# Unnormalised band, sums divided out at the readout, and first x as fp32 over one queue: a fused convolution and gated FFN on one Trainium2 core

## Chip, core and metric

One core of a Trainium2 chip runs the kernel. The metric is device time in microseconds (us) of one execution. Of the kernel before, three runs gave 765.75, 765.9 and 766.1 us.

## What is computed

`x` is 8 sequences of 4096 tokens with 192 channels. A causal convolution with 7 taps, one set of taps for each of 8 heads of 24 channels, is followed by a gated feed-forward layer with 1536 hidden channels. The taps are a softmax over the 7 weights of a head.

```python
w = np.exp(weight - np.max(weight, axis=-1, keepdims=True))
w = w / (np.sum(w, axis=-1, keepdims=True) + 1e-09)
...
out = np.einsum('hk,bskhg->bshg', w, x_unf)        # 7 taps, group = D // H = 24
...
gate = np.maximum(x @ w_gate, 0.0)
val = x @ w_val
return (gate * val @ w_out).astype(np.float32)
```

## The kernel before

The eight sequences are two streams of four (sequence b and b + 4 side by side). The work goes in 16 units of 1024 tokens of both streams, each of two windows of 512. For a window, `gate_val` (L528) runs twelve blocks f of 128 hidden channels. A block is 12 matmuls (L541): three channel blocks c of 64 channels, two streams, gate and val; the two streams use the upper and lower half of the array, so the weights `Wg` and `Wv` are held twice, in partitions 0 to 63 and 64 to 127. ACT takes the ReLU of gate (L552), DVE multiplies by val (L553). `project` (L636) multiplies by `Wo` (L570) and ACT and DVE evict.

The convolution of most tokens runs on DVE, ACT and POOL as products and sums with the taps (`lane_first`, `lane_rest`, `product`, `add`), one unit ahead. The first unit has nothing ahead of it, so its convolution runs on PE, as matmuls with a **band matrix**: x in token-major form (`x_h`) is the weight and the band, 118 x 112 with the 7 taps along its diagonals, one for each head, is the moving operand; the result comes out channel-major. Its first window is `first_block` (L387), the second window `second_block` (L394, in front of block f = 5), and the tail of unit 1 is `conv(2)` (L403) with `conv_out` (L421). A window of the first block is cut in 5 token steps jj: step 0 has 96 tokens, steps 1 to 4 have 104 each.

The order of work is written by hand: every engine runs its instructions in the order of the program text, and waits on semaphores. All psum tiles come from one pool of 4 buffers (L71). What stands before the first gate matmul:

- **Taps and band** (L249 to L299): SP loads the weights; DVE takes the maximum (L251), ACT the exp (L254), DVE the sum, the reciprocal and `over`, the reciprocals on a diagonal (L258 to L261). An fp32 matmul of exp and `over` (L272) spreads the normalised taps over 112 partitions; DVE multiplies them into `diag` (L282); 14 matmuls (L292) shift them into the band in psum; `fill_band` (L323) copies it to SBUF as 16 bit.
- **x of the first window**: SP loads steps 1 to 4 of stream 0 as fp32 in one transfer (L122, 336 KB) and step 0 of both streams (L138); ACT (L317) and DVE (L335) cast them to 16 bit. POOL loads steps 1 to 4 of stream 1 with the cast in the transfer (L127).
- **POOL's queue**: after that issue, a mask (L128), and then the issues of the weight pieces s = 0 to 5 (`load_w`, L167) and of x for the second block (`load_x(1)`), with copies of the upper halves (`pool_halves`, L179) between. DVE makes the upper halves of pieces 0 and 1 (`both_halves`, L175), which serve block 0 and blocks 1 and 2; POOL those of piece 2 (blocks 3 and 4) and up.
- **Warm-ups** (L152): matmuls on constants, seven ahead of the taps' matmul and two more between.
- **Taps for the lane** (L303 to L314): ACT scales the exps; ten SP transfers spread them over partitions (`tap`); POOL copies them to the other half (L665). They are read from unit 1's convolution on.

In the first block, channel block 0 takes stream 0 of steps 1 to 4, then stream 1, then step 0; channel blocks 1 and 2 follow. Each block is read from psum to `xc` by one copy of 512 columns (L392): blocks 0 and 2 by ACT, block 1 by DVE.

## Time and profile before

| what | us |
|---|---|
| median of three runs | 765.9 |
| profiled execution, first to last instruction (span) | 764.4 |
| PE busy | 760.3 |
| DVE busy | 705.6 |
| ACT busy | 600.9 |
| POOL busy | 378.4 |
| first convolution matmul starts at | 5.65 |
| first gate matmul starts at | 7.66 |

The profile gives one execution. Its rows have a line of the kernel, an engine, an operation, the tile written and the tiles read; PEld is the loading of weights into PE, which runs beside its matmuls. An idle time in brackets is followed by what ended it. The granted TensorE clock is shown as 9 tenths or more in every slice of the page.

### The profile page before, as it was taken

Reading aid. Unit: us, or ns where it says so; the run is one execution under the profiler, and the core shown is the slowest. Engines: PE = TensorE matmul, PEld = TensorE weight load, DVE = VectorE, ACT = ScalarE, POOL = GpSimd, SP = SyncE. Lnnn points to the kernel's source line nnn. Section 1 sums busy time; section 2 is a strip of 40 time slices with the busy share of each in tenths; the row PEclk is TensorE's granted clock in tenths of the full one; section 3 lists DMA queues with packets and bytes.
Section 4 is the critical chain, followed back from the end, with each engine's and each line's share of the span. In section 5 each row is a group of like instructions: output and inputs, shape, how many; then the busy total and the mean of one; then the engine's idle time right before and its main releaser. Section 6 shows DMA issues by size and latency. Waiting matters only on the chain.

```text
span 764.4 us, 25103 instructions
## 1 busy us (share of the span) xinstructions
PE 760.3 (99%) x10929; PEld 501.3 (66%) x10929; DVE 705.6 (92%) x763; ACT 600.9 (79%) x735; POOL 378.4 (50%) x244
## 2 busy tenths in 40 slices
PE   9999999999999999999999999999999999999998
PEld 5494674947649476584855848567494674947648
DVE  7998999999999999999999999999999999999891
ACT  6787887878878887887878878787787887876571
POOL 9419448093571926729175390853909347090000
PEclk9999999999999999999999999999999999999999
DMA  9969039290452805528073271722819134220202
GB/s 123 134 102 148 7 96 81 65 111 22 95 67 83 97 23 107 49 85 94 30 112 40 85 94 44 120 16 90 89 44 125 13 97 60 66 48 15 71 1 84
DMA packets 131830, 56.00 MB, mean 73 GB/s; under 512 B 96392, under 2 KB 131720, under 8 KB 131720
## 3 DMA queue, kind: packets, MB, share of 16 engines
q1 hardware_dynamic: 90680, 38.81, 23.9%
q0 software_dynamic: 40896, 15.50, 20.3%
q8 instruction: 85, 1.39, 0.8%
q14 instruction: 25, 0.20, 0.1%
q10 hardware_dynamic: 144, 0.10, 0.0%
HBM read 31.48 MB, written 25.17 MB: 74 GB/s over the span
## 4 chain that ended last, share of the span: by engine, by line
PE 99%; DVE 0%; ACT 0%; issue 0%
PE ps L541 65%; PE ps L570 32%; PE ps L619 1%; PE ps L377 0%; PE ps L154 0%; PE ps L411 0%; DVE band L329 0%; PE ps L272 0%; ACT acc L596 0%; PE ps L292 0%
## 5 line engine op out<-in xcount | busy, mean ns | idle before, releaser
L553 DVE TENSOR_TENSOR hT<-gr,ps 128x1024 f16<-128x1024 f16 (+1 forms) x386 | 469.0, 1216 | 36.6 <-ACT gr L552 9.4
L552 ACT ACTIVATE gr<-ps 128x1024 f16<-128x1024 f32 (+1 forms) x386 | 392.9, 1019 | 101.9 <-PE ps L541 99.7
L491 POOL TENSOR_TENSOR prods<-prods 128x1344 f32<-128x1344 f32 x70 | 212.4, 3034 | 290.0 <-DVE prods L487 286.7
L541 PE MATMUL ps<-xc,Wg 64*128 64x512 f16 x2304 | 311.9, 376 | 0.0
L541 PE MATMUL ps<-xc,Wv 64*128 64x512 f16 x2304 | 311.9, 376 | 0.0
L570 PEld LDWEIGHTS <-hT 64*128 64x128 f16 x5952 | 245.9, 94 | 3.7
L570 PE MATMUL ps<-Wo,hT 64*128 64x192 f16 x5952 | 248.1, 243 | 0.0
L541 PEld LDWEIGHTS <-Wv 64*128 64x128 f16 x2304 | 129.8, 94 | 118.5 <-DVE hT L553 0.3
L541 PEld LDWEIGHTS <-Wg 64*128 64x128 f16 x2304 | 112.3, 94 | 132.8 <-issue 0.2
L515 DVE SCALAR_TENSOR_TENSOR acc<-x_r,tap,acc 128x576 f32<-128x576 f16 x225 | 165.3, 813 | 0.0
L485 ACT ACTIVATE prods<-x_r,tap 128x448 f32<-128x448 f16 x222 | 130.1, 660 | 0.0
L596 ACT COPY out_s<-ps 128x768 f32<-128x768 f32 (+1 forms) x64 | 45.5, 711 | 51.3 <-PE ps L570 40.0
L203 POOL DMA_DIRECT2D x_e<-in_x_dram x58 | 47.0, 823 | 16.6 <-ACT acc L501 12.8
L465 POOL COPY x_p<-x_e 128x960 f16<-128x960 f16 (+1 forms) x58 | 50.3, 906 | 1.2 <-DMA x_e<-in_x_dram 1.1
L491 POOL TENSOR_TENSOR xc<-prods 128x1344 f16<-128x1344 f32 x14 | 42.4, 3029 | 1.1
L515 DVE SCALAR_TENSOR_TENSOR xc<-x_r,tap,acc 128x576 f16<-128x576 f16 x45 | 34.1, 813 | 0.0
L501 ACT ACTIVATE acc<-x_r,tap 128x576 f32<-128x576 f16 x45 | 31.4, 763 | 0.0
L487 DVE TENSOR_SCALAR prods<-x_r,tap 128x448 f32<-128x448 f16 x70 | 26.6, 450 | 0.0
L596 DVE COPY out_s<-ps 128x384 f32<-128x384 f32 (+1 forms) x16 | 8.7, 541 | 11.9 <-PE ps L619 9.4
L619 PE MATMUL ps<-Wo,hT 128*128 128x192 f16 x96 | 8.1, 246 | 0.0
L619 PEld LDWEIGHTS <-hT 128*128 128x128 f16 x96 | 7.9, 98 | 0.2 <-issue 0.2
L154 PE MATMUL ps<-const-bfloat16-1.0 128*128 128x512 bf16 (+1 forms) x9 | 3.9, 572 | 0.8 <-PEq L719 0.8
(54 smaller groups left out, 56.3 us busy)
## 6 DMA issues: line engine op xcount, KB each, us to landing
out_dram<-out_s SPq DMA_DIRECT2D x62, 384.0 KB, 2.7
x_e<-in_x_dram POOLq DMA_DIRECT2D x34, 192.0 KB, 7.4
x_e<-in_x_dram POOLq DMA_DIRECT2D x24, 240.0 KB, 5.6
x_r<-x_p SPq DMA_TRANSPOSE x131, 5.1
Wo<-in_moe_w_out_dram POOLq DMA_DIRECT2D x1, 576.0 KB, 7.3
x_h<-in_x_dram POOLq DMA_DIRECT2D x2, 210.0 KB, 4.8
Wg<-in_moe_w_gate_dram POOLq DMA_DIRECT2D x4, 96.0 KB, 4.1
Wv<-in_moe_w_val_dram POOLq DMA_DIRECT2D x4, 96.0 KB, 4.0
```

Source lines behind the costliest of these rows:

```text
L203: first = nc.gpsimd.dma_start(out=xe[:, j0 + start : j0 + n, st, :, :].rearrange("p j c r -> p j (c r)"), in_=bass.AP(tensor=x.tensor, off ...
L465: nc.gpsimd.tensor_copy(out=xp[:, j0 : j0 + n, :, st, :], in_=xe[:, j0 : j0 + n, st, :, :])
L485: engine.activation(out=out, in_=in_, func=ACTF.Copy, scale=scale)
L487: engine.tensor_scalar(out=out, in0=in_, scalar1=scale, scalar2=None, op0=ALU.mult)
L491: nc.gpsimd.tensor_tensor(out=pr[:, 0] if k < KW - 1 else xc[v + 1][:, :, LDVE:UNIT], in0=pr[:, 0], in1=pr[:, k], op=ALU.add,)
L501: nc.scalar.activation(out=accs[v][:, c, :], in_=shifted(v, c, 0, 0), func=ACTF.Copy, scale=tap[:, c, 0:1],)
L515: nc.vector.scalar_tensor_tensor(out=xc[v][:, c, 0:LDVE] if k == KW - 1 else acc[:, c, :], in0=shifted(v, c, k, 0), scalar=tap[:, c, k : k ...
L541: nc.tensor.matmul(out=pss[i][:, st, :], lhsT=W[64 * st : 64 * st + 64, c, 128 * f : 128 * (f + 1)], rhs=xcb[64 * st : 64 * st + 64, c, WI ...
L552: nc.scalar.activation(out=gr[:, sts], in_=pss[0][:, sts], func=ACTF.Relu)
L553: nc.vector.tensor_tensor(out=h[:, f, sts], in0=gr[:, sts], in1=pss[1][:, sts], op=ALU.mult)
L570: mm = nc.tensor.matmul(out=outs[q], lhsT=h[64 * r : 64 * r + 64, f, st, 128 * q : 128 * (q + 1)], rhs=Wo[64 * r : 64 * r + 64, f, :], sta ...
L596: one(out=dst[:, step * j : step * j + step], in_=src[:, step * j : step * j + step])
```

## The change

- The exps go into the band **unnormalised**: ACT writes them as 16 bit (`high`), and a 16-bit matmul with a one-hot matrix spreads them. Sum, reciprocal and `over` are made later; four fp32 matmuls (`spread_scales`) put the reciprocals into all 128 partitions, by channel and by head, and the copies out of psum multiply by them (`by_channel`, and ten scaled copies in `conv_out` in place of five copies).
- `diag` is made in two halves, the band in two psum tiles and copied in four pieces of two heads (before: 3, 1, 2 and 2).
- x of the first window comes **as fp32 by SP alone**: one transfer for each token step of both streams (`load_first`, 168 KB each), in the order 1, 2, 0, 3, 4. Each is cast by one instruction: steps 1 and 3 by ACT, 2 and 4 by DVE, 0 by POOL between its weight issues.
- POOL no longer issues x of stream 1. It makes `owner` and `owners` (a one at each channel's head) with two selects and a copy ahead of the weight issues.
- The first block runs steps 1 and 2 for all three channel blocks, then `spread_scales`, then step 0 with a readout of columns 0 to 303, then the upper halves of weight piece 0 on DVE, then steps 3 and 4 with a readout of columns 304 to 511.
- Four warm-ups of 512 columns stand ahead of the taps' matmul (before: six of 512 and one of 256), 256 columns behind it and 512 behind the band.
- The lane's taps and their ten SP transfers come after the first block.

The diff, without what is only moved:

```diff
-    def body(st):
...
+    def load_first(jj):
+        nc.sync.dma_start(
+            out=stage(0, SUB, 0, 2, jj, 1),
+            in_=bass.AP(
+                tensor=x.tensor,
+                offset=x.offset + (FIRST - PAD + DSUB * (jj - 1)) * D,
+                ap=[[D, SUB], [NB * S * D, 2], [1, D]],
+            ),
         )
 
-    nc.sync.dma_start(out=stage(0, SUB, 0, 1, 1, GSUB - 1), in_=body(0))
+    load_first(1)
+    load_first(2)
+    ones = const.tile([128, 128], FP)
-    nc.gpsimd.dma_start(out=xts[0][0:SUB, 1:GSUB, 1, :], in_=body(1))
...
+    owner = const.tile([H, D], FP)
+    for sign in (1, -1):
+        nc.gpsimd.affine_select(
+            out=owner[:],
+            in_=ones[0:H, 0:1].to_broadcast([H, D]) if sign == 1 else owner[:],
+            pattern=[[sign, D]],
+            compare_op=ALU.is_ge,
+            fill=0.0,
+            base=0 if sign == 1 else G - 1,
+            channel_multiplier=-G * sign,
+        )
+    owners = const.tile([H, NCH, 2, 64], FP)
+    nc.gpsimd.tensor_copy(
+        out=owners[:],
+        in_=owner[:].rearrange("h (c r) -> h c r", r=64).unsqueeze(2).to_broadcast([H, NCH, 2, 64]),
+    )
...
+    load_first(3)
+    load_first(4)
...
     def warm_up(*widths):
-        for n, w in enumerate(widths):
+        for w in widths:
             nc.tensor.matmul(
-                out=warm[:, n % 2, 0:w], lhsT=busy[:, 0:128], rhs=busy[:, 0:w], start=True, stop=True
-            )
-
-    warm_up(512, 512, 512, 512, 512, 512, 256)
+                out=warm[:, 0, 0:w], lhsT=busy[:, 0:128], rhs=busy[:, 0:w], start=True, stop=True
+            )
+
+    warm_up(512, 512, 512, 512)
...
+    def cast(copy, jj):
+        rows = ROWS0 if jj else FIRST + PAD
+        copy(out=xts[0][0:rows, jj, :, :], in_=stage(0, rows, 0, 2, jj, 1))
+
     load_w(0)
-    load_w(1)
+    load_w(1, 1)
+    cast(nc.gpsimd.tensor_copy, 0)
+    load_w(1, 2)
...
+    same = const.tile([SUB, SEG], FP)
+    summed(same[:], pitch_k, SEG, GAP)
+    one_hot = const.tile([H, H], F16)
+    nc.vector.tensor_copy(out=one_hot[:], in_=spaced[0:H, 0, GAP : GAP + H])
     mx = const.tile([H, 1], FP)
     nc.vector.tensor_reduce(
         out=mx[:], in_=wr[:], axis=mybir.AxisListType.X, op=ALU.max, negate=True
     )
+    high = const.tile([H, KW, SEG], F16)
     nc.scalar.activation(
-        ex[:, 0:KW, :], wr[:].unsqueeze(2).to_broadcast([H, KW, SEG]), ACTF.Exp, bias=mx[:]
+        high[:], wr[:].unsqueeze(2).to_broadcast([H, KW, SEG]), ACTF.Exp, bias=mx[:]
     )
+    nc.scalar.activation(ex[:, 0:KW], wr[:], ACTF.Exp, bias=mx[:])
+    summed(places[:, SUB - SEG : SUB - SEG + SEG + KW - 1], pitch_k - 1, SEG + KW - 1, GAP)
+    nc.tensor.matmul(
+        out=warm[0:SUB, 1, 0:H],
+        lhsT=high[:].rearrange("h k s -> h (k s)"),
+        rhs=one_hot[:],
+        start=True,
+        stop=True,
+    )
+    warm_up(256)
+    HB = H // 2
+    diag = const.tile([SUB, H, SEG], F16)
...
+            nc.vector.tensor_tensor(
+                out=diag[:, HB * a : HB * (a + 1)],
+                in0=warm[0:SUB, 1, HB * a : HB * (a + 1)].unsqueeze(2).to_broadcast([SUB, HB, SEG]),
+                in1=same[:].unsqueeze(1).to_broadcast([SUB, HB, SEG]),
+                op=ALU.mult,
+            )
+    bps = [psum.tile([128, 2, 512], FP, name="ps") for _ in range(2)]
...
     sm = const.tile([H, 1], FP)
-    nc.vector.tensor_reduce(out=sm[:], in_=ex[:, :, 0], axis=mybir.AxisListType.X, op=ALU.add)
+    nc.vector.tensor_reduce(out=sm[:], in_=ex[:], axis=mybir.AxisListType.X, op=ALU.add)
+    fill_band(0, [0, 1], nc.vector.tensor_copy)
+    fill_band(0, [2, 3], nc.vector.tensor_copy)
+    fill_band(1, [4, 5], nc.scalar.copy)
+    fill_band(1, [6, 7], nc.scalar.copy)
+    cast(nc.scalar.copy, 1)
+    cast(nc.vector.tensor_copy, 2)
     nc.vector.reciprocal(sm[:], sm[:])
...
+    scales = const.tile([128, NCH + H], FP)
+
+    def spread_scales():
+        for c in range(NCH):
             nc.tensor.matmul(
-                out=(bps, spread)[a][:, a, HB * SEG * b : HB * SEG * (b + 1)],
-                lhsT=places[:, SUB - SEG * (b + 1) : SUB - SEG * (b + 1) + 128],
-                rhs=diag[:, HB * a : HB * (a + 1), :].rearrange("p h s -> p (h s)"),
+                out=bps[1][:, 1, c : c + 1],
+                lhsT=owners[:, c].rearrange("h a b -> h (a b)"),
+                rhs=sm[:],
                 start=True,
                 stop=True,
                 skip_group_check=True,
             )
+        nc.tensor.matmul(
+            out=bps[1][:, 1, NCH : NCH + H],
+            lhsT=ones[0:H, :],
+            rhs=over[:],
+            start=True,
+            stop=True,
+            skip_group_check=True,
         )
+        nc.scalar.copy(out=scales[:], in_=bps[1][:, 1, 0 : NCH + H])
+
+    def scaled(engine, out, in_, scale):
+        if engine is nc.scalar:
+            engine.activation(out=out, in_=in_, func=ACTF.Copy, scale=scale)
+        else:
+            engine.tensor_scalar(out=out, in0=in_, scalar1=scale, scalar2=None, op0=ALU.mult)
+
+    def by_channel(engine, out, in_, c):
+        scaled(engine, out, in_, scales[:, c : c + 1])
...
-    def conv_dense(g, c, ps, bank):
+    def conv_dense(g, c, ps, bank, steps):
...
+        for jj in steps:
...
     def first_block():
-        for c in range(NCH):
-            ps = psum.tile([128, 2, 512], FP, name="ps")
-            conv_dense(0, c, ps, 0)
-            copy = nc.vector.tensor_copy if c == 1 else nc.scalar.copy
-            copy(out=xc[0][:, c, 0:WIN], in_=ps[:, 0, :])
+        xc[0] = xcpool.tile([128, NCH, UNIT], F16, name="xc")
+        place = [(psum.tile([128, 2, 512], FP, name="ps"), 0) for _ in range(NCH)]
+        cut = GROUPS[0][1][3]
+        engines = (nc.scalar, nc.vector, nc.scalar)
+        for steps, done in (((1, 2), None), ((0,), slice(0, cut)), ((3, 4), slice(cut, WIN))):
+            for c, (ps, bank) in enumerate(place):
+                conv_dense(0, c, ps, bank, steps)
+                if done is not None:
+                    by_channel(engines[c], xc[0][:, c, done], ps[:, bank, done], c)
+            if done is None:
+                spread_scales()
+            elif done.start == 0:
+                both_halves(nc.vector.tensor_copy, 0, Wg)
+                both_halves(nc.vector.tensor_copy, 0, Wv)
...
+        conv_dense(1, 0, two, 0, range(GSUB))
+        conv_dense(1, 1, two, 1, range(GSUB))
+        for c in range(2):
+            by_channel(nc.scalar, xc[0][:, c, WIN : 2 * WIN], two[:, c], c)
+        conv_dense(1, 2, one, 0, range(GSUB))
+        by_channel(nc.vector, xc[0][:, 2, WIN : 2 * WIN], one[:, 0], 2)
...
+        for h, (t, bank, slot) in PLACE.items():
+            r = G * h
+            while r < G * (h + 1):
+                c, m = r // 64, min(64 - r % 64, G * (h + 1) - r)
+                scaled(
+                    nc.scalar,
+                    y[0:SUB, 0:n, c, :, r % 64 : r % 64 + m],
+                    wide[t][0:SUB, bank, W * slot : W * (slot + 1)].rearrange(
+                        "p (j s w) -> p j s w", s=2, w=G
+                    )[:, :, :, r - G * h : r - G * h + m],
+                    scales[0:SUB, NCH + h : NCH + h + 1],
+                )
+                r += m
...
     first_block()
+    taps = const.tile([H, KW], FP)
+    nc.scalar.activation(taps[:], ex[:, 0:KW], ACTF.Copy, scale=sm[:])
+    tap = const.tile([128, NCH, KW], FP)
...
+            nc.sync.dma_start(
+                out=tap[r % 64 : r % 64 + n, c, :],
+                in_=taps[h : h + 1, :].unsqueeze(1).to_broadcast([1, n, KW]),
+            )
```

## The prediction

> **What bounds the kernel now.** I read the page first, parts 1 and 4, and then the chain that ended last, in order of time. PE is busy nearly the whole span, and the chain is PE from end to end:

> ```profile
> span 764.4 us, 25103 instructions
> PE 760.3 (99%) x10929; PEld 501.3 (66%) x10929; DVE 705.6 (92%) x763; ACT 600.9 (79%) x735; POOL 378.4 (50%) x244
> PE 99%; DVE 0%; ACT 0%; issue 0%
> ```

> ```profile
> 0.85 2.93 PE ps L154 x7
> 3.78 0.47 PE ps L272 x2
> ...
> 4.79 0.27 PE ps L292 x7
> ...
> 5.09 0.52 DVE band L329
> ...
> 5.65 2.08 PE ps L377 x106
> 7.72 6.66 PE ps L541 x60
> 14.38 1.48 PE ps L377 x120
> 15.86 24.74 PE ps L541 x228
> ...
> 57.46 31.08 PE ps L541 x288
> ```

> Columns: start, length, engine, tile, line. From 7.72 us on PE only multiplies; 288 gate/val matmuls take 31.08 us everywhere, so one block f (12 of them) takes 1.295 us. From there to the end the change removes no matmul, and for the first window PE needs 5 blocks x 1.295 = 6.48 us where the chain shows 6.66. So this change can only move the **time at which gate/val begins** (call it T0; 7.66 in the timeline below), and add or take away stalls in the few blocks behind it, where weights arrive just in time. What lies outside the span is 765.9 - 764.4 = 1.5 us; I keep it, so that the sum, made against the span, carries over to the median.

> The prologue on DVE, ACT and PE (timeline; start, length, what, in brackets the idle time before it):

> ```profile
> 2.10 0.20 ACT L145 ACTIVATE spare<-ones 8x1 f32<-8x1 f32 x1
> 2.19 0.15 DVE L251 TENSOR_REDUCE mx<-wr 8x1 f32<-8x7 f32 x1 [0.47 <-DMA wr<-in_weight_dram]
> 2.37 0.39 ACT L254 ACTIVATE ex<-wr,mx 8x112 f32<-8x112 f32 x1
> ...
> 3.39 0.35 DVE L238 TENSOR_REDUCE same<-spaced 112x16 f32<-112x112 f32 x1
> ...
> 4.29 0.29 DVE L282 TENSOR_TENSOR diag<-ps,same 112x128 f16<-112x128 f32 x1 [0.20 <-PE ps L272]
> ...
> 4.63 0.62 PE L292 MATMUL ps<-diag,places 112*128 112x64 f16 x14
> ...
> 5.09 0.51 DVE L329 CAST band<-ps 128x336 f16<-128x336 f32 x1 [0.51 <-PE ps L292]
> ...
> 5.12 0.92 ACT L317 CAST x_h<-prods 110x256 f16<-110x256 f32 x2 [1.60 <-DMA prods<-in_x_dram]
> ...
> 5.65 2.08 PE L377 MATMUL ps<-band,x_h 110*32 110x104 f16 x120 [0.18 <-DVE band L329]
> 5.67 0.36 DVE L335 CAST x_h<-prods 102x384 f16<-102x384 f32 x1
> ...
> 5.95 0.27 DVE L329 CAST band<-ps 128x112 f16<-128x112 f32 x1
> 5.96 0.58 ACT L329 CAST band<-ps 128x224 f16<-128x224 f32 x2
> 6.18 1.38 PEld L377 LDWEIGHTS <-x_h 110*32 110x32 f16 x104 [0.15 <-DMA x_h<-in_x_dram]
> ...
> 6.86 0.59 ACT L392 CAST xc<-ps 128x512 f16<-128x512 f32 x1 [0.32 <-PE ps L377]
> ...
> 7.66 0.39 PE L541 MATMUL ps<-xc,Wg 64*128 64x512 f16 x2
> ```

> Two waits end late here: the taps' chain (exp, sum, reciprocal, spread, diag, band) lets the convolution begin at 5.65; the second stream's x, loaded by POOL, holds it from 6.0 to 6.18.

> **Part by part: the taps' chain, to the first convolution.** Sum, reciprocal and `over` leave the chain. The exp now feeds a 16-bit matmul directly: exp done at 2.76, or some 0.05 later since `same` (0.35) and a tiny copy now stand ahead of the maximum on DVE, instead of behind `over`. PE has only four warm-ups of 2.93 / 6.5 = 0.45 us ahead, free at 2.65, so the matmul runs at about 2.85 and ends near 3.2. Diag in halves: 0.29 for 128 elements, so about 0.2 for 64: first half 3.45, second 3.6. Fourteen band matmuls: seven take 0.27 us on the chain (39 ns each) at the faster rate, and 64/512 x 0.45 = 56 ns each at the warm-ups' rate; the rate may change among them, so I take 50 ns, 0.7 us for all, and 0.2 us, an estimate, until the last can be read. First half readable near 4.15, second at 4.5.

> ACT then copies band 4-5 and 6-7 (0.58 together) and casts step 1 of x: 384 elements, half of the 768 that took 0.92, so 0.46 to 0.5: 4.55 + 0.58 + 0.47 = 5.6. DVE has its two bands (between 0.27 for 112 and 0.51 for 336, so 0.39 each) and the cast of step 2 (0.36) at 5.2 to 5.3. So the convolution begins at **about 5.6, against 5.65**: the chain is shorter by 0.9 us, but the cast that stood ahead of ACT's bands now stands behind them. x itself is not what holds. The issues of before, with size and time to landing:

> ```profile
> Wv<-in_moe_w_val_dram POOLq DMA_DIRECT2D x4, 96.0 KB, 4.0
> prods<-in_x_dram SPq DMA_DIRECT2D x1, 336.0 KB
> x_h<-in_x_dram POOLq DMA_DIRECT2D x1, 168.0 KB, 4.7
> prods<-in_x_dram SPq DMA_DIRECT2D x1, 144.0 KB, 4.0
> ...
> Wv<-in_moe_w_val_dram POOLq DMA_DIRECT2D x1, 48.0 KB, 3.4
> ```

> Steps 1 and 2 are 336 KB as that first transfer was, which ended ACT's wait at 5.12, and stand in the same place of the same queue. All five transfers read the 816 KB that passed by 6.18 before (POOL's 168 KB were 336 as read); with the weights issued later beside them I put step 4 at 5.9 (5.6 to 6.2) and its cast on DVE at 6.3.

> **Part by part: the convolution and its readout.** PE's order becomes steps 1, 2 (48 matmuls), spread_scales, step 0 (24), steps 3, 4 (48). At 1.48 us for 120, as in the second block, 48 take 0.6: done at 6.2. Then four fp32 matmuls with 128 columns of weights. The one fp32 matmul of before (L272, 112 columns, two records) holds PE for 0.47 at the warm-ups' rate, 0.24 at double rate; four of them 0.9 us. Bounds: 4 x 0.47 = 1.9 us, and 0.5 if weight loads and products of neighbours overlap. I take **0.9: done at 7.1**. This work did not stand in PE's queue before, and everything behind it waits.

> Step 0's cast is on POOL and done by about 6.2 (below), so it is hidden behind this. ACT reads the scales (0.20, as the tiny copy at 2.10) from 7.3 to 7.5. Then channel block 0, columns 0 to 303: 304/512 x 0.59 = 0.35 to 0.4, to 7.95. Steps 3 and 4 write other columns of the same bank, but in the changed program's order of instructions their first matmul for each block waits for that readout's engine. So PE goes on with block 0 at 8.0, 16 matmuls 0.2, 0.2 until readable, then ACT again (it did block 2's first part meanwhile): 208 columns, 0.3: 8.7. **T0 = 8.75 against 7.66, +1.1.** Before, the last convolution of block 0 ended at 6.8 and one copy of 0.59 followed. Block 1 on DVE stands behind both weight copies, block 2 behind block 0 on ACT; they are needed 0.45 and 0.9 us after T0 and come within that.

> **Part by part: POOL and the weights.**

> ```profile
> 1.42 0.88 POOL L127 DMA_DIRECT2D x_h<-in_x_dram  x1 [0.28 <-issue]
> ...
> 2.39 0.36 POOL L128 TENSOR_SCALAR_AFFINE_SELECT spaced<-ones 112x112 f32<-112x112 f32 x1
> ...
> 4.59 0.63 POOL L170 DMA_DIRECT2D Wv<-in_moe_w_val_dram  x1
> ...
> 9.62 6.43 DVE L553 TENSOR_TENSOR hT<-gr,ps 128x512 f16<-128x512 f16 x7 [0.67 <-ACT gr L552]
> ...
> 10.14 0.82 POOL L177 COPY Wv<-Wv 64x768 f16<-64x768 f16 x1
> ...
> 12.27 0.81 PE L541 MATMUL ps<-xc,Wv 64*128 64x512 f16 x6
> ...
> 23.03 0.25 POOL L665 COPY tap<-tap 64x21 f32<-64x21 f32 x1
> ```

> POOL loses the issue of x (0.88) and gains two selects of 192 elements and a copy of 384. Between 0.25 for 21 elements and 0.82 for 768 a straight line gives 0.38 and 0.53; the select of 112 lies 0.04 above it. So 2 x 0.42 + 0.53 - 0.88 = +0.5 (bounds 3 x 0.25 - 0.88 = -0.1 and 3 x 0.82 - 0.88 = +1.6). Behind it the first three weight issues; then the cast of step 0 waits for its x (landed before DVE's cast at 5.67; the same bytes ahead of it in the queue now) and takes 0.53: the issue of the second Wv piece starts at 6.0 against 4.59, **+1.4 for all of POOL's later work**. The upper-half copy of Wv for blocks 3 and 4 ends at 10.96 + 1.4 = 12.4; block 3's val matmuls wanted it at 12.27. With T0 at 8.75 they come at 13.3, so this is hidden; with T0 unchanged it would cost 0.1. DVE's products start at 9.62, behind the ReLU and behind the copy of that second Wv piece; issued at 6.0, it lands 3.4 to 4.0 later, so 9.4 to 10.0, its copy (0.5, by the same line) ends at 9.9 to 10.5. With T0 at 8.75 the first products would start at 9.62 + 1.1 = 10.7. Hidden too; with T0 unchanged up to 0.9 late.

> What else moves is free: the taps and their ten SP issues come behind the first block but are used at 23.03. The second block's two readouts on ACT instead of one, and ten scaled copies instead of five after conv(2), come where ACT waits for PE and not PE for ACT, as at the end of that unit:

> ```profile
> 57.54 0.48 ACT L596 COPY out_s<-ps 128x384 f32<-128x384 f32 x1 [1.23 <-PE ps L570]
> ```

> Five more copies at 0.2 each would be 1.0 us, less than this idle time; without the cover they would cost that.

> **Sum:** +1.1 for T0; of the 0.1 us that blocks 1 to 3 lose now, 0.1 is won back, since DVE and POOL are no longer late. **+1.0: span 765.4, 766.9 us.**

> **The clock at the start.** The warm-ups take 0.45 us per 512 columns, the steady pairs 2 x 31.08/288 = 0.216, and the change of rate falls among the L292 matmuls, near 4.7, after 3.9 us in which PE never stood idle. Now it stands idle from about 2.65 to 2.85 and 3.2 to 3.5; I take it that the rate still changes near 4.7. [...]

> **Rivals.** (1) *Everything as above*: 766.9, from 766.5 to 767.9 by the bounds of the fp32 matmuls (T0 8.35 to 9.75 alone, and 0.3 to either side from transfers). Chance 0.55.

> (2) *The start moves little*: the fp32 matmuls pass in 0.5 us, the first convolution starts 0.3 earlier, and the readouts overlap better. T0 is then about 7.7, and POOL's 12.4 decides: +0.1, 766.0; if the late Wv piece holds DVE as well, up to +0.9, 766.8. For it: it takes only small errors in steps that I added up in a row. Chance 0.2.

> (3) *Faster*: x and the band come early enough that T0 is 7.2, and POOL's delay is under 1.0 (select and copy near 0.25, step 0's x landed before its turn): gain 0.3 to 0.5, 765.5. It decides from a POOL delay under 1.3, since block 3 is held otherwise. Against it: the serial readout alone is 1.5 us long. Chance 0.1.

> (4) *Much slower*: the gaps keep PE at half rate past 5.6. If the 3.9 us of unbroken work that went before the change of rate must be counted anew from 3.5, it comes at 7.4, and half of the 1.8 us since 5.6 is lost: 0.9 on top of +1.0, 767.8. If it lasts through, 48 convolutions cost 0.6 more, the fp32 matmuls 0.95 and the next 40 0.5: 768.9. It decides where the fourteen band matmuls and the first 48 convolutions run at half rate. Chance 0.15.

> **How the numbers follow.** The likeliest is (1), 766.9. The range from 765.6 to 768.2 leaves out about half of (3), a third of (4) and little else. A measurement of this kernel tells about 0.2% (1.5 us, 764.4 to 767.4) from no change. Faster than that would need T0 at 6.1, before the x of the last steps is cast: 0.02. Slower: nearly all of (4) and a fifth of (1), 0.25. Within: 0.73.

> **What would show it.** In the changed profile: the first convolution near 5.6; the four fp32 matmuls holding PE for 0.9 us; each of steps 3 and 4 waiting for ACT or DVE; the first gate matmul at 8.75; the second Wv issue at 6.0 on POOL; from then on blocks of 1.295 us. It is wrong if gate/val begins before 8 us, if blocks 1 to 4 stall, or if the convolution's 120 matmuls run at half rate.

## The result and the profile after

| | before | after |
|---|---|---|
| median, us | 766.02 (765.75 to 766.21) | 771.09 (770.38 to 771.67, five runs) |
| ratio, 95% interval | | 1.0065 [1.0052, 1.0077] |
| profiled execution / its span | 766.1 / 764.4 | 770.38 / 768.7 |
| first convolution matmul / first gate matmul (T0) | 5.65 / 7.66 | 5.68 / 10.84 |

Slower by 5.07 us, where 1.0 was forecast; 771.09 lies above the range. (The 766.1 is inferred: in every run on record that has both, 1.7 us of the time lie outside the span, and of the three runs of before only 766.1 fits 764.4.) The page of after looks as the one of before did: span, PE's busy time, and the granted clock in 40 slices.

```profile
span 768.7 us, 25130 instructions
...
PE 763.1 (99%) x10933; PEld 502.1 (65%) x10933; DVE 706.7 (92%) x767; ACT 602.8 (78%) x745; POOL 379.0 (49%) x247
...
PEclk9999999999999999999999999999999999999999
```

None of it tells what happened: a slice is 19 us long, and matmuls that run more slowly count as busy for longer (a pair of gate matmuls 0.43 us in place of 0.21, below). The chain of waits of after does (start, length, engine, tile, line):

```profile
2.80 0.25 PE ps L291
3.05 0.34 PE ps L175
...
3.41 0.24 DVE diag L303
...
3.69 0.92 PE ps L312 x14
...
4.63 0.59 ACT band L329 x2
5.22 0.42 ACT x_h L244
...
5.68 1.23 PE ps L412 x45
6.92 1.37 PE ps L358 x6
8.29 0.43 PE ps L366 x2
8.72 0.31 PE ps L412 x7
...
9.11 0.52 ACT xc L378
...
9.68 1.23 PE ps L412 x36
10.91 7.47 PE ps L578 x60
18.38 1.48 PE ps L412 x120
```

The second block begins at 18.38 against 14.38: 4.00 us lost by then, 3.19 of them ahead of the first gate matmul (10.91 against 7.72) and 0.81 among the next 60 matmuls (7.47 against 6.66). Nothing is lost after that; the same piece of the chain 500 us later stands 4.00 later too, in before and in after:

```profile
510.82 15.84 PE ps L570 x384
```

```profile
514.82 15.84 PE ps L607 x384
```

The other 0.3 us of the span come behind the last copy out of psum, which starts 4.00 us later too (765.40 against 761.40). The timeline of after shows what the 0.81 us are, and when x and the weights came (idle time before and its end in brackets):

```profile
5.68 1.23 PE L412 MATMUL ps<-band,x_h 110*32 110x104 f16 x48 [0.67 <-ACT x_h L244]
...
5.74 0.50 POOL L244 CAST x_h<-prods 102x384 f16<-102x384 f32 x1 [0.89 <-DMA prods<-in_x_dram]
6.20 0.64 POOL L191 DMA_DIRECT2D Wv<-in_moe_w_val_dram  x1
...
6.46 0.51 ACT L244 CAST x_h<-prods 110x384 f16<-110x384 f32 x1 [0.82 <-DMA prods<-in_x_dram]
...
6.93 0.36 DVE L244 CAST x_h<-prods 110x384 f16<-110x384 f32 x1 [1.41 <-DMA prods<-in_x_dram]
...
10.84 0.61 PE L578 MATMUL ps<-xc,Wg 64*128 64x512 f16 x2
...
12.10 0.64 PE L578 MATMUL ps<-xc,Wv 64*128 64x512 f16 x2
12.52 0.43 PE L578 MATMUL ps<-xc,Wg 64*128 64x512 f16 x2
12.79 0.38 PE L578 MATMUL ps<-xc,Wv 64*128 64x512 f16 x2
13.00 0.81 PE L578 MATMUL ps<-xc,Wg 64*128 64x512 f16 x6
```

A pair of gate matmuls takes 0.43 us from start to start (12.10 to 12.52) until about 12.6 and 0.21 behind it (12.79 to 13.00): **PE ran at half its rate until 12.6 us**, where before it changed near 4.8. The 48 convolution matmuls at 5.68 took 1.23 us, not 0.6. This is rival (4) of the prediction, but longer than that rival allowed.

### The profile page after: what moved, and what is told of

The parts are those of the page before. It is cut to its first block, busy times and chain, and to the rows that moved or that the text cites. A ratio compares the mean times of both kernels' runs of the same rounds, so it can differ in the third digit from the quotient of the medians.

```text
span 768.7 us, 25130 instructions
## 1 busy us (share of the span) xinstructions
PE 763.1 (99%) x10933; PEld 502.1 (65%) x10933; DVE 706.7 (92%) x767; ACT 602.8 (78%) x745; POOL 379.0 (49%) x247
## 4 chain that ended last, share of the span: by engine, by line
PE 99%; ACT 0%; DMA 0%; issue 0%; DVE 0%; ACTq 0%
PE ps L578 65%; PE ps L607 32%; PE ps L656 1%; PE ps L412 1%; PE ps L358 0%; DMA wr<-in_weight_dram 0%; PE ps L312 0%; PE ps L456 0%; ACT band L329 0%; ACT xc L378 0%; PE ps L366 0%; ACT x_h L244 0%; ACT high L286 0%; PE ps L175 0%; ACT acc L633 0%
## 5 line engine op out<-in xcount | busy, mean ns | idle before, releaser
L552 DVE SCALAR_TENSOR_TENSOR acc<-x_r,tap,acc 128x576 f32<-128x576 f16 x225 | 165.3, 812 | 0.0
L552 DVE SCALAR_TENSOR_TENSOR xc<-x_r,tap,acc 128x576 f16<-128x576 f16 x45 | 34.0, 812 | 0.0
L412 PE MATMUL ps<-band,x_h 110*32 110x104 f16 (+7 forms) x240 | 4.7, 247 | 1.0 <-ACT x_h L244 0.7
## 6 DMA issues: line engine op xcount, KB each, us to landing
prods<-in_x_dram SPq DMA_DIRECT2D x4, 168.0 KB, 3.8
```

What stands on the lines that cost most here:

```text
L552: nc.vector.scalar_tensor_tensor(out=xc[v][:, c, 0:LDVE] if k == KW - 1 else acc[:, c, :], in0=shifted(v, c, k, 0), scalar=tap[:, c, k : k ...
```

## What could be the cause, and how it shows

| window that ran at half rate | share, and the run |
|---|---|
| half rate kept | 0.47 and 0.41 (after), 0.76, 0.62, 0.58 (e1), 0.54 (e3), 0.46, 0.74 (e4), 0.72 (e9), 0.70 (e8) |
| full rate granted | 0.82 (before, e8), 0.82 (after, 9.2 to 12.6), 0.78 (e10), 0.85 (e2), 0.87 (e9), 0.89 (e5, e6, e7), 0.90 (e11), 0.93 (e3), 0.96 (e4), 1.00 (e1) |

| window that ran at full rate | share, and the run |
|---|---|
| full rate kept | 0.81 (before), 0.71 (e11), 0.56 (e7), 0.54 (e6), 0.53 (e10), 0.50 (e5) |
| full rate taken away | 0.37 (e2), 0.20 (e8) |

The measure is chosen to fit these windows; the busy time of the profile does not part them. In the window of after from 5.79 to 9.20 PE is busy for 3.41 of 3.41 us, the four fp32 matmuls included, and half rate is kept.

*Theory*: the change opens gaps on PE while it still works at half rate (fewer warm-ups, 0.32 us of waiting for `diag`, 0.67 in front of the convolution, 1.44 us with three fp32 matmuls of one column), so the share is 0.47 and 0.41 in two windows, below the 0.76 behind which e1, too, stays at half rate. *Rivals*: the unnormalised band with its scales is dear by itself; x over one queue comes late; the serial readout.

## The experiments

**e1, e2: fill the gaps in after.** e1 adds warm-ups on both sides; e2 also gives the taps' matmul a psum tile of its own (in after it sits in the warm-up's tile, and `diag` waits for the warm-up behind it).

```diff
-    warm_up(512, 512, 512, 512)
+    warm_up(512, 512, 512, 512, 256)
...
+    spread = psum.tile([128, 2, 512], FP, name="ps")        # e2 alone
-        out=warm[0:SUB, 1, 0:H],
+        out=spread[0:SUB, 0, 0:H],
-    warm_up(256)
+    warm_up(384)                                            # e2 alone
...
-    warm_up(512)
+    warm_up(512, 512, 512)
```

> The changed kernel with more warm-ups: 256 columns more ahead of the taps' matmul, and three instead of one of 512 columns behind the band, so that PE stands idle before the first convolution only for some 0.3 us at 3.4. Theory 'clock' (the idle stretches at 2.7, 3.4 and 5.0 to 5.7 keep PE at half rate until 12.6): the rate doubles by about 6, the four fp32 matmuls take 0.9 instead of 1.80 us, the 48 first convolutions 0.6 instead of 1.23, first gate matmul near 9.0 instead of 10.84, about 767.3. Theory 'added work' (the fp32 matmuls and the split readout cost the same at any rate): no change, 771.

> As e1_fill, and the taps' matmul writes a psum tile of its own instead of a bank of the warm-up tile, so that diag does not wait for the warm-up behind it; that warm-up has 384 columns. PE has no idle stretch over 0.1 us before the first convolution. Theory 'clock': the rate doubles no later than in e1_fill, near 4.8; band 0.3 us earlier, but the casts of x still hold the first convolution near 5.4 to 5.7; about 767.0. Theory 'added work': 770.7 (0.3 for the shorter chain).

Measured: e1 770.02 us, 1.0042 [1.0029, 1.0054], its runs from 767.83 to 771.56. The profiled one is the slowest; in it T0 is 11.04, and the rate changes only at 14.9, against the theory's 6. Its window up to 4.68 had 0.76, and half rate stayed; the lowest share with full rate behind it is e10's 0.78. e2 768.42, 1.0036 [1.0024, 1.0048]: full rate at 4.75, the 48 convolutions 0.66 us (5.56 to 6.22) and the fp32 matmuls 0.98 (6.22 to 7.20). And then the windows of e2 show what neither theory had: columns are stretch, length, busy us (and instructions) of PE, PEld, DVE, ACT and POOL, then the granted clock, the DMA share and GB/s.

```profile
4.80:8.10 3.30, 2.61 (x83) 1.88 (x82) 1.32 (x6) 1.90 (x7) 2.82 (x6) 1.00 1.04 159
8.20:11.50 3.30, 3.30 (x60) 1.76 (x61) 1.91 (x6) 1.36 (x4) 3.26 (x6) 0.50 1.19 134
11.60:15.00 3.40, 3.40 (x36) 1.39 (x32) 2.56 (x5) 3.09 (x5) 3.35 (x6) 1.00 1.37 166
```

The full rate was **taken away again** at 8.16, after a window in which PE waited for ACT's readouts and did fp32 matmuls. So the serial middle of after did not keep the rate that the fills had won. (The first stretch of a trace, ahead of any change of rate, is shown as 1.00 even where it is half: so in before from 1.0 to 4.7, where warm-ups of 512 columns start 0.43 us apart. There only the lengths tell.)

**e3: before, with one gap.**

```diff
-    warm_up(512, 512, 512, 512, 512, 512, 256)
+    warm_up(512, 512, 512, 512)
```

> The kernel before with four warm-ups of 512 columns ahead of the taps' matmul instead of six and one of 256: one edit, PE idle from 2.6 to 3.7, all else as before. Theory 'clock': the rate doubles one or two windows of some 3.4 us later than 4.8, at 8.2 or 11.6; 120 convolutions and the first gate blocks at half rate cost 1.0 to 3.0 us, 767 to 769. Theory 'added work': 766.0, as nothing waits for the removed matmuls.

Measured: 767.08 us, 1.0016 [1.0006, 1.0025]. The timeline of e3:

```profile
3.63 0.51 PE L272 MATMUL ps<-over,ex 8*112 8x8 f32 x2 [0.92 <-ACT taps L304]
...
5.77 3.08 PE L377 MATMUL ps<-band,x_h 110*32 110x104 f16 x120
8.78 0.39 PE L541 MATMUL ps<-xc,Wg 64*128 64x512 f16 x2
```

The same arithmetic as before, and PE idle for 0.92 us: half rate lasts until 8.82, the convolution takes 3.08 us for 2.08, and T0 moves by 1.1. Three warm-ups that compute nothing are worth 1.1 us.

**e4: 16-bit matmuls for the scales, in after.**

```diff
-    owners = const.tile([H, NCH, 2, 64], FP)
+    owners = const.tile([H, NCH, 2, 64], F16)
...
+    sm_h = const.tile([H, 1], F16)
+    nc.vector.tensor_copy(out=sm_h[:], in_=sm[:])
-    over = const.tile([H, H], FP)
+    over = const.tile([H, H], F16)
...
-                rhs=sm[:],
+                rhs=sm_h[:],
-            lhsT=ones[0:H, :],
+            lhsT=ones_h[:],
```

> The changed kernel with the four matmuls that spread the scales in 16 bit instead of fp32 (one-hot matrices, reciprocals and their diagonal rounded to 16 bit; two tiny DVE instructions more). Theory 'added work': the 1.80 us of the four fp32 matmuls fall to about 0.3, 769.6. Theory 'clock': the same 1.5 us in the prologue, and whether the rate doubles earlier depends on what the step counts as activity; if the fp32 matmuls with one column count as idle, the rate doubles at 9.2 instead of 12.6, and some 768.

Measured: 769.22 us, 1.0042 [1.0026, 1.0058]. The timeline of e4:

```profile
6.86 0.23 PE L362 MATMUL ps<-sm_h,owners 8*128 8x1 f16 x3
6.96 0.16 PE L370 MATMUL ps<-over,ones_h 8*128 8x8 f16 x1
7.05 0.67 PE L416 MATMUL ps<-band,x_h 102*32 102x96 f16 x24
...
9.24 0.61 PE L582 MATMUL ps<-xc,Wg 64*128 64x512 f16 x2
```

0.19 us for the four instead of 1.80 (6.85 to 8.65 in after), and T0 is 1.6 earlier; the time, 1.9 below after's, is near the 769.6 of 'added work'. The rate still changes only at 12.5. So the fp32 matmuls are dear by themselves too: at full rate, in e2, they still take 0.98, and the other 0.8 of their 1.80 is the rate.

**e5, e6, e7: hold the rate through the middle.** e5 is e2 with two matmuls on constants between step 0 and steps 3 and 4; e6 is e2 with e4's 16-bit scales and three such fills; e7 is e6 with one fill and one readout of 512 columns for each channel block, behind steps 3 and 4.

```diff
+            for w in (512, 512):                            # e5; e6 three, e7 one
+                nc.tensor.matmul(
+                    out=bps[1][:, 0, 0:w], lhsT=busy[:, 0:128], rhs=busy[:, 0:w],
+                    start=True, stop=True, skip_group_check=True,
+                )
...
-                if done is not None:                        # e7 alone
-                    by_channel(engines[c], xc[0][:, c, done], ps[:, bank, done], c)
+                if steps[0] == 3:
+                    by_channel(engines[c], xc[0][:, c, 0:WIN], ps[:, bank, :], c)
```

> As e2_fill_all, with two matmuls of 512 columns on constants between step 0 and steps 3 and 4, where PE waited 0.6 us for the readout; fp32 matmuls stay. In e2_fill_all the granted clock fell back to 0.50 from 8.16 to 11.58 after a window (4.75 to 8.16) in which PE streamed columns for 0.37 of the time. Theory 'clock share' (a window of 3.41 us counts as busy from about 0.8 of it on, and a window near 0.4 takes the full rate away): the window has now 0.5 to 0.55; if that holds the rate, T0 8.6 to 9.0 and 766.9 to 767.3 in every run; if it doesn't, as e2_fill_all, 767.6 to 771. Theory 'added work': 768.4 as e2_fill_all or a little more.

> As e2_fill_all, with the scales spread by 16-bit matmuls and three matmuls of 512 columns on constants between step 0 and steps 3 and 4. Theory 'clock share': at full rate all along, first gate matmul near 8.4 (the cast of step 4 ends near 7.2, one more readout behind it), 766.7 with little spread. Theory 'added work': the fp32 matmuls gone, what is left is the split readout, 766.8; so this run shows the sum of both mends, and the spread of its times whether the rate is held.

> As e6_fill_16 with one readout of 512 columns for each channel block behind steps 3 and 4 in place of two, and one matmul on constants instead of three. PE no longer waits for ACT and DVE between the steps. If the split readout costs what it seems to in the changed kernel (0.6 us between step 0 and step 3 at PE), T0 is near 8.1 and the time 0.2 to 0.4 below e6_fill_16; if step 4's x (landed 6.9) is what holds, the longer readout (0.75 for 0.43) makes it 0.1 to 0.3 slower than e6_fill_16.

Measured: 768.08 (1.0027 [1.0016, 1.0038]), 767.86 (1.0025 [1.0015, 1.0036]) and 767.56 us (1.0026 [1.0017, 1.0036]). All three keep the full rate once they have it (shares 0.50, 0.54 and 0.56 in the table); T0 is 9.53, 8.82 and 8.67. e5 and e6 are 0.8 to 1.2 us slower than expected: e5 has the full rate only from 6.72 on, and in e6 x is late. e7's T0 was put near 8.1. The timelines of e5 and, behind it, of e7:

```profile
5.54 1.23 PE L413 MATMUL ps<-band,x_h 110*32 110x104 f16 x48
...
9.53 0.39 PE L588 MATMUL ps<-xc,Wg 64*128 64x512 f16 x2
```

```profile
5.42 0.73 PE L417 MATMUL ps<-band,x_h 110*32 110x104 f16 x48
...
6.51 0.51 ACT L246 CAST x_h<-prods 110x384 f16<-110x384 f32 x1 [1.15 <-DMA prods<-in_x_dram]
...
7.14 0.38 PE L440 MATMUL ps<-const-bfloat16-1.0 128*128 128x512 bf16 x1 [0.43 <-ACT scales L379]
7.45 0.73 PE L417 MATMUL ps<-band,x_h 110*32 110x104 f16 x48
8.67 0.39 PE L591 MATMUL ps<-xc,Wg 64*128 64x512 f16 x2 [0.48 <-ACT xc L383]
```

e5 computes the same as after, fp32 matmuls included, and adds work to PE. In the profiled executions it is 2.14 us faster (768.24 against 770.38): T0 comes 1.31 earlier, and the 60 matmuls behind it take 6.68 us again, for 7.47. Its convolution begins at 5.54, which is 0.14 of it. So some 2.0 of the 4.3 us that separate the traces of before and after are the clock, and it would be more with the full rate throughout, since e5's first 48 convolutions still take 1.16. The median of e5 alone doesn't decide, as 'added work' had 768.4; the record of the rate does. By the medians e5 is 3.0 us faster; the other 0.9 stands in no trace. That e5 keeps the rate in every execution fits its spread: 0.6 us over seven, where e2's seven have 3.5.

What remains in e7, 1.5 us, isn't clock. Its T0 is 1.0 late: ACT's cast of step 3 waits for x until 6.51, the scales' copy stands behind it, and then come the fill, steps 3 and 4 and a readout. The 228 matmuls behind the second block lose 0.2 (24.93 for 24.74), and the end of the span, behind the last copy, another 0.2. e7 is 0.3 below e6, but it has both one readout in place of two and two fills fewer, so the price of the split readout is not shown apart.

**e8, e10: the loading of x alone.** e8 is before with after's five transfers on SP and a cast for each step (1 and 3 ACT; 0, 2 and 4 DVE), in the order of steps 1, 2, 0, 3, 4; band and readouts are before's. e10 lets POOL cast step 0, between the weight issues, so that four of the six transfers of pieces 0 to 2 wait for x.

```diff
-    nc.sync.dma_start(out=stage(0, SUB, 0, 1, 1, GSUB - 1), in_=body(0))
+    load_first(1)
+    load_first(2)
...
-    nc.gpsimd.dma_start(out=xts[0][0:SUB, 1:GSUB, 1, :], in_=body(1))
...
+    load_first(3)
+    load_first(4)
...
     load_w(0)
+    cast(nc.gpsimd.tensor_copy, 0)                          # e10 alone
     load_w(1)
```

> The kernel before with the new loading of x alone: five fp32 transfers on SP in the order 1, 2, 0, 3, 4, casts of steps 1 and 3 on ACT, 2, 0 and 4 on DVE, convolution steps in that order with both streams; normalised band, warm-ups and single readouts as before. Step 4 landed at 6.9 in the changed kernel, against 6.18 for the last x before. Theory 'clock': the warm-ups are as before, so PE has the full rate from 4.8, and the cost is that of the later x: T0 8.2 to 8.5, 766.6 to 766.9. Theory 'added work' with the loading as its main part: 769 to 770.

> The run with the new loading of x put into the kernel before (median 770.84), with one edit: POOL casts step 0 of x, which waits for its landing, between the issues of the first and the second weight pieces, so that two instead of six weight transfers are under way while x is loaded. Theory (x came late there because the weight transfers on POOL's queue share the DMA engines with it): step 0 is cast at 5.5 to 6.2 instead of 7.3, step 3 at 6.3 to 7 instead of 8.38, step 4 at 6.8 to 7.6 instead of 9.30; T0 8.5 to 9.5, full rate kept or lost for one window; 767 to 769, the second weight piece landing near 10.5 and holding block 1. Rival (the five transfers on SP's queue are slow by themselves): casts within 0.4 us of 7.3, 8.4 and 9.3, and 770 or more.

Measured: e8 770.84 us, 1.0072 [1.0051, 1.0092], a miss by 4 us. Its profiled execution is the slowest of its four, 773.92 us; the others took 770.18 to 771.12. Its timeline, and e10's (768.61, 1.0037 [1.0020, 1.0053]) behind it:

```profile
7.30 0.36 DVE L127 CAST x_h<-prods 102x384 f16<-102x384 f32 x1 [1.14 <-DMA prods<-in_x_dram]
...
8.38 0.51 ACT L127 CAST x_h<-prods 110x384 f16<-110x384 f32 x1 [2.22 <-DMA prods<-in_x_dram]
...
9.30 0.50 DVE L127 CAST x_h<-prods 110x384 f16<-110x384 f32 x1 [1.64 <-DMA prods<-in_x_dram]
```

```profile
6.54 0.50 POOL L127 CAST x_h<-prods 102x384 f16<-102x384 f32 x1 [3.33 <-DMA prods<-in_x_dram]
...
6.73 0.51 ACT L127 CAST x_h<-prods 110x384 f16<-110x384 f32 x1 [0.56 <-DMA prods<-in_x_dram]
...
7.32 0.47 DVE L127 CAST x_h<-prods 110x384 f16<-110x384 f32 x1 [1.16 <-DMA prods<-in_x_dram]
```

With fewer weights under way the same five transfers bring steps 0, 3 and 4 at 6.5, 6.7 and 7.3 instead of 7.3, 8.4 and 9.3. So x came late in e8 because of the weights on POOL's queue. Why they mattered less in before is argued, not shown: POOL's issue of x, 0.88 us long, had held them back, and with that gone they began at 1.74 instead of 2.67. After itself fits: three weight transfers, begun at 2.76, left the same steps at 5.74, 6.46 and 6.93, earlier than two begun at 1.73 did in e10. Fewer transfers on POOL's queue brought SP's 0.8 to 2.0 us earlier; how the one holds up the other, no run here shows. In e8 PE then waits so long for x that the full rate is lost from 8.8 to 15.6 and T0 is 11.86; in e10 T0 is 8.99 at full rate, but the 60 matmuls behind it take 7.14 us for 6.66: the groups of six that start at 13.03 and 13.76 take 0.73 and 0.77 us until the next one begins, where the one at 10.39 takes 0.65.

**e9, e11: the band's form alone.** Before, with its own loading of x and order of convolution, but unnormalised exps in 16 bit, 16-bit scales behind channel block 0, scaled readouts and warm-ups laid anew.

```diff
-        lhsT=ex[:, 0:KW, :].rearrange("h k s -> h (k s)"),
-        rhs=over[:],
+        lhsT=high[:].rearrange("h k s -> h (k s)"),
+        rhs=one_hot[:],
...
-            copy(out=xc[0][:, c, 0:WIN], in_=ps[:, 0, :])
+            if c == 0:
+                spread_scales()
+            by_channel(nc.vector if c == 1 else nc.scalar, xc[0][:, c, 0:WIN], ps[:, 0, :], c)
```

> The kernel before, with x loaded and cast as before and the order of its convolution as before, and only the band's half of the change: unnormalised exps through a 16-bit matmul with the one-hot matrix, sums and reciprocals behind them, scales spread by four 16-bit matmuls behind channel block 0, scaled readouts. The warm-ups are laid so that PE streams without a long gap (as in the fill experiments), owners are made by POOL behind its first four weight issues. Theory (the clock and the way x is loaded carry the loss, not the band's form): full rate from about 4.8 on and held, first convolution 5.5, second stream's x still lands at 6.2, T0 8.0 to 8.3 (the scales' matmuls, their copy of 0.16 and a readout of 0.69 for 0.59), time 766.2 to 766.9. Rival (the unnormalised form is dear by itself: scales, scaled readouts and POOL's owners): T0 8.7 or later, 767.5 or more, at full rate.

> The band's form alone once more, with one thing mended: in the run before, DVE made the lane matrix (same) and the one-hot matrix ahead of the maximum, and both wait for POOL's mask, which in this loading of x ends at 2.75; so the maximum came at 3.14 instead of 2.19, the taps' matmul at 3.84, and PE stood still for 0.92 us ahead of it and kept half rate until 10.15. Here the maximum comes first, and the fills are 2432 columns ahead of the taps' matmul and 1152 behind it. Theory (clock and loading of x carry the loss): full rate from 4.8 on and held, first convolution 5.3 to 5.6, T0 7.9 to 8.4, time 766.2 to 766.9. Rival (the unnormalised form is dear by itself): full rate as well, but T0 8.7 or later and 767.5 or more.

Measured: e9 767.82 us, 1.0017 [1.0008, 1.0027], against both expectations' clock: its timeline shows a gap of the experiment's own making, and half rate until 10.15 (0.72 in the window up to 6.74).

```profile
3.84 0.25 PE L283 MATMUL ps<-one_hot,high 8*112 8x8 f16 x1 [0.92 <-ACT high L277]
...
6.59 1.37 PE L433 MATMUL ps<-band,x_h 110*32 110x104 f16 x40
...
9.92 0.49 PE L591 MATMUL ps<-xc,Wg 64*128 64x512 f16 x2
```

e11, with the maximum first on DVE and more warm-ups: 766.83 us, 1.0006 [0.9997, 1.0016], full rate from 4.83 on.

```profile
2.98 0.23 PE L283 MATMUL ps<-one_hot,high 8*112 8x8 f16 x1
...
5.59 0.54 PE L433 MATMUL ps<-band,x_h 110*32 110x104 f16 x16
...
6.44 0.63 PE L433 MATMUL ps<-band,x_h 110*32 110x104 f16 x24 [0.30 <-DMA x_h<-in_x_dram]
...
8.22 0.39 PE L591 MATMUL ps<-xc,Wg 64*128 64x512 f16 x2
```

As the theory said, T0 8.22 and within 766.2 to 766.9. The taps' matmul runs 0.7 us earlier than before's (2.98 against 3.71), and the convolution begins at 5.59 against 5.65: the shorter chain wins next to nothing, since x is what is waited for (ACT's cast waits for it until 4.95, PE for 0.30 us at 6.44). By the medians the unnormalised form with 16-bit scales is 0.8 us slower here, but the interval includes no difference. No version was faster than before by its median.

## Why the prediction was wrong

**The step that failed** is in "The clock at the start": "I take it that the rate still changes near 4.7". The gaps were seen (2.65 to 2.85 and 3.2 to 3.5) and their size was about right, but the 0.67 us in front of the convolution were not counted; the sum put the effect of all of them at nothing, and the longest case in the rivals ended it 40 matmuls behind the fp32 ones. In after the window up to 5.79 had a share of 0.47, the next one, up to 9.20, 0.41, and only the third, in which steps 3 and 4 and the gate matmuls run, 0.82. That rival lacked one thing: the middle of the new order, with its fp32 matmuls of few columns and its waits, has a share of only 0.41 itself, and half rate stays behind it too.

By the prediction's own steps, T0 from 8.75 to 10.84:

- **First convolution 5.6**: 5.68, +0.08. The chain went as worked out, up to ACT's cast behind its bands.
- **48 convolutions 0.6 us**: 1.17 until the next matmul, +0.57; 0.67 at full rate (e7: 5.42 to 6.09).
- **Four fp32 matmuls 0.9 us**: 1.80, +0.90. The full-rate figure was good (0.98 in e2); the upper bound of 1.9 was the half-rate one.
- **From there to T0, 1.65 us**: 2.19 (8.65 to 10.84), +0.54. At full rate e5 takes 1.85 (7.68 to 9.53), so 0.34 of it is steps 0, 3 and 4 at half rate and 0.2 was mis-sized, the readouts above all (0.51 for 0.35 to 0.4, 0.43 for 0.3). That they wait for the readout's engine was right (0.36 for ACT).
- **First blocks -0.1**: +0.81 against before, half rate until 12.6.
- **x of step 4 landed 5.9 (5.6 to 6.2)**: the wait for it ended at 6.93, a miss. The bytes in its own queue don't set the time alone; the weights beside them count as well (the same five transfers had step 4 cast at 9.30 in e8 and at 7.32 in e10). In after the fp32 matmuls hid it. In e6 and e7 the late x does decide T0, by way of step 3 (cast at 6.54 and 6.51, ahead of the scales' copy).
- **POOL +1.4**: second Wv issue 6.20 for 6.0, right, and hidden as said, because T0 was so late. With T0 at 8.8, in e6, it was not: DVE waited 1.09 us for that piece, and a weight load 0.36 for DVE's copy (at 11.04).

At full rate the sum of the prediction comes near. The nearest to its kernel is e5, T0 9.53, which keeps fp32; without the 0.5 that its first 48 convolutions lose at half rate that is 9.0, an estimate, against 8.75. That e6 and e7 have 8.82 and 8.67 is chance: with 16-bit scales they lack the 0.9 of the fp32 matmuls, and x that came late takes its place. The time of the three is 767.6 to 768.1 rather than 766.9. Rival (4) named the mechanism, and its two times, 767.8 and 768.9, were too short by 3.3 and 2.2 us. Its first case had the rate change at 7.4; in after windows end at 5.79, 9.20 and 12.62, and the change came with the third.

The 1.5 us outside the span were 1.7: 765.9 is the median and 764.4 the span of another execution. The forecast, a difference to the median, isn't moved by it. The 0.2 us until a last product can be read, taken twice in the sum, is the author's estimate and stands in no row: in after ACT's copies start 0.02 us (4.63) and 0.08 us (9.11) behind the end that the profile gives their matmuls (4.61 and 9.03).

**What stays open.** The median lies 0.7 us above the profiled execution of after, its fastest, and e1's runs spread over 3.7 us. For e1 and e8 the profiled execution is the slowest. Where the windows lie against the kernel's start differs between profiled executions (by the recorded changes, reckoned back by 3.41 us where the change came later, a window ends at 4.78 in before, 5.79 in after, 5.40 in e3 and e8, 6.72 in e5), which could make such a spread, but single executions other than the profiled ones left no trace. The last 0.3 us of the span, behind the last copy, were not followed.

## What to carry to other kernels

While PE is not yet at its full rate, idle time can cost more than itself: with e3's 0.92 us half rate lasts until 8.82, and T0 comes 1.1 us later. In these runs full rate came behind windows of 3.41 us with an estimated share of streamed columns of 0.78 and more, and not behind 0.76 and less; so reckon that share anew for each edit of a prologue, by columns, of which the four fp32 matmuls have eleven in 1.80 us. A busy share of 99% and a clock row of nines hid it in after; read the rate off the length of a known matmul. And a transfer that moves to another queue releases what stood behind it (in e8 the first weights are issued at 1.74 for 2.67): look at what now runs beside the critical one.

## What the runs showed of the hardware that was not expected

- **The full rate is lost without any long pause**: in e2 the window with 0.37 has no idle time of PE over 0.51 us in it, 2.61 of 3.30 us were busy in the profile's sense, and half rate follows from 8.16 to 11.58.
- **The shares differ by direction**: by the estimates in the tables above, a window at half rate was followed by full rate from 0.78 (e10) up and not at 0.76 (e1) and below; one at full rate kept it from 0.50 (e5) up and lost it at 0.37 (e2) and 0.20 (e8).
- **fp32 matmuls of one to eight columns are dear, and PE loads weights nearly all of that time**: 1.80 us for four at half rate (after) and 0.98 at full (e2), against 0.19 and 0.18 for four in 16 bit (e4 and e7). PEld is busy for 1.35 of the 1.44 us of the first three in after, six loads of 0.28 to 0.33 us that overlap; at full rate the six take 0.74 us together in e2, and the three loads of the 16-bit ones 0.14 in e7.
